# Seven products for every out block, first raw products in single banks, and a rewritten order of steps, in a fused attention and gated-unit kernel

## The chip, the cores and the metric

The kernel runs on one core of a Trainium2 chip. The metric is device time in microseconds (us) for one launch. Five engines work side by side, each on its own queue in strict program order: TensorE (PE, with weight loads listed as PEld), VectorE (DVE), ScalarE (ACT), GpSimd (POOL) and SyncE (SP, which here only issues transfers). They wait for one another by semaphores.

## What is computed

Eight batches, eight heads, 576 tokens, head size 64, all in fp32. First an attention without softmax, normalised per token and head; then a gated unit whose gate is a causal convolution over 5 tokens:

```
kv  = einsum('bhsd,bhse->bhde', k, v)
out = einsum('bhsd,bhde->bhse', q, kv)
x   = out / sqrt(mean(out*out, -1) + 1e-6) * g_norm     # heads side by side: (8, 576, 512)
gate = sigmoid(sum over taps k of conv_w[k] * x shifted by 4-k tokens)
result = (gate * (x @ w_val)) @ w_out                   # (8, 576, 512)
```

## The kernel before

**Tiling.** A batch `b` has five token chunks `c`: four of 128 tokens and one of 64. Channels are cut into four blocks `jt` of 128. Tokens lie strided, so that the convolution's shifts are shifts by 32 columns. The 64-token chunks of two batches share one out block; a pair of batches is numbered `i`, and its nine out blocks `c` 0 to 8.

**Steps.** Every piece of work is a small function, and a long list of step names, `PLAN`, calls them in an order written out in full (1151 steps). Engines follow that order strictly, so the list is the schedule. For one batch the steps are:

- `load_half`, `load_q`: k, v and q from memory (SP's queue). `turn_q` transposes q on VectorE (L458, L461); for batches 0 and 1 `turn_q_rows` does it on TensorE.
- `kv_product` (L438, TensorE) and `kv_copy` (ScalarE): k times v per head.
- `raw_product` (L493) or, from batch 2 on, `raw_pair` (L510): q times kv. A pair writes two chunks into a PSUM tile of two banks, `raws`. In batches 0 and 1 chunks 3 and 2 write one half each of the same tile.
- `square` (ScalarE), `sums` (L540, VectorE), `powers` (L546, GpSimd), `normalise` (ScalarE, 8 small activations; VectorE in batch 0).
- `turn_blocks` (L600, VectorE) and `move_blocks` (L608, four transfers from GpSimd's queue) bring x to channels by tokens, `xT`; `halo` copies the columns before it. Batches 0, 1 and the short chunks go by `turn_x` and `keep_x`.
- `gate_start` (L619, ScalarE), four `gate_tap` (L625, VectorE), `gate_end` (L632, ScalarE, sigmoid), `gated` (L650, VectorE: gate times value into `gv`).
- `val_product`, `keep_val` for batches 0 and 1; from batch 2 on the seven-product form: `x_sums` (L671, VectorE) forms sums of token halves, `val_fast` (L687) multiplies, `val_keep` copies or adds the results.
- `out_product` (L718, L725 for the shared short chunk) with `keep_out` (L733) for pairs `i` 0 and 1. For pairs 2 and 3 the seven-product form: `token_sums` (L758, VectorE), `fast_product` (L784, TensorE), `fast_keep` (L793 to L808: four copies on ScalarE and three adds on VectorE), with weight sums made once by `weight_sums`. Then `store`.

**The seven-product form.** Two out blocks of 128 tokens are one product of a 2 by 2 block matrix by a 2 by 2 block matrix. Instead of eight half-size products it makes seven, of sums and differences. A full block takes four products with 512 columns; a pair of blocks in the other form takes seven times two products with 256 columns. The number n of a `fast_product i p n` tells which of the seven, and p which pair of blocks.

**Buffers.** `gv` holds the gated values of three batches in turn. PSUM has eight banks: `raws` takes two, tag "tp" one and tag "mm" five, handed out by pools in the order of the calls; near the end `raws` is given back for two more. Work tiles (`gate` three, `ot` three, `x` two, `xs` four, `w64` three) come from pools too. The weights arrive in 64-bit form and are narrowed to fp32 by `narrow_weight` in eight small steps each, five on VectorE and three on ScalarE.

Of the kernel before, what the change touches and what calls it, by code (L numbers as in the profile page):

```python
# [15 lines left out]
P = 128  # L16
# [3 lines left out]
load_q_rows 0 1; stage_weight cw 0; load_q_rows 0 0; load_half v 0 0; load_half k 0 0; load_half v 0 1;  # L20
load_half k 0 1; warm_up; stage_weight wval 1; stage_weight wval 0; start_warm 36; turn_q_rows 0 0;
turn_q_rows 0 1; narrow_weight cw 0 0; turn_q_rows 0 2; narrow_weight cw 0 1; narrow_weight cw 0 2; sort_q 0 0;
turn_q_rows 0 3; sort_q 0 1; turn_q_rows 0 4; narrow_weight cw 0 3; kv_product 0 0; sort_q 0 2;
load_q_rows 1 0; narrow_weight cw 0 4; narrow_weight cw 0 5; load_half k 1 0; sort_q 0 3; narrow_weight cw 0 6;
load_half v 1 0; narrow_weight cw 0 7; sort_q 0 4; load_q_rows 1 1; load_half k 1 1; stage_weight wval 2;
keep_warm 2; kv_product 0 1; stage_weight wval 3; turn_cw; load_half v 1 1; kv_copy 0; keep_cw;
narrow_weight wval 1 0; raw_product 0 3; load_half v 2 0; raw_product 0 2; square 0 3; raw_product 0 4;
sums 0 3; stage_weight wout 0; square 0 2; raw_product 0 1; square 0 4; powers 0 3; sums 0 2;
narrow_weight wval 1 1; sums 0 4; raw_product 0 0; load_half v 2 1; square 0 1; narrow_weight wval 0 0;
narrow_weight wval 0 1; powers 0 2; square 0 0; normalise 0 3; sums 0 1; turn_x 0 3; sums 0 0; keep_x 0 3;  # L30
powers 0 4; normalise 0 2; narrow_weight wval 1 2; narrow_weight wval 1 3; turn_x 0 2; normalise 0 4;
turn_q_rows 1 0; roots 0; keep_x 0 2; narrow_weight wval 0 2; turn_x 0 4; sort_q 1 0; turn_q_rows 1 1;
keep_x 0 4; narrow_weight wval 0 3; normalise 0 1; turn_q_rows 1 2; halo 0; sort_q 1 1; normalise 0 0;
turn_x 0 1; narrow_weight wval 1 4; kv_product 1 0; narrow_weight wval 0 4; keep_x 0 1; sort_q 1 2;
narrow_weight wval 0 5; turn_x 0 0; narrow_weight wval 1 5; narrow_weight wval 0 6; turn_q_rows 1 3;
keep_x 0 0; narrow_weight wval 0 7; gate_start 0 0; turn_q_rows 1 4; narrow_weight wval 1 6; kv_product 1 1;
sort_q 1 3; load_q 2 0; narrow_weight wval 1 7; gate_start 0 1; narrow_weight wval 2 0; val_product 0 0 1;
gate_start 0 2; narrow_weight wval 3 0; sort_q 1 4; load_q 2 1; gate_tap 0 2 3; kv_copy 1; gate_tap 0 0 3;
narrow_weight wval 3 1; raw_product 1 3; narrow_weight wval 2 1; gate_tap 0 1 3; load_half k 2 0;
raw_product 1 2; keep_val 0 0 1; gate_tap 0 0 2; square 1 3; narrow_weight wval 3 2; val_product 0 1 1;  # L40
sums 1 3; square 1 2; gate_tap 0 1 2; powers 1 3; narrow_weight wval 2 2; load_half k 2 1; gate_tap 0 2 2;
narrow_weight wval 2 3; stage_weight wout 2; raw_product 1 1; sums 1 2; narrow_weight wval 3 3;
narrow_weight wval 2 4; raw_product 1 0; keep_val 0 1 1; powers 1 2; square 1 1; narrow_weight wval 2 5;
normalise 1 3; val_product 0 0 0; load_q 2 2; gate_tap 0 0 1; sums 1 1; turn_q 2 0; normalise 1 2; powers 1 1;
turn_x 1 3; narrow_weight wval 3 4; val_product 0 1 0; narrow_weight wval 2 6; keep_x 1 3; load_q 2 3;
narrow_weight wval 3 5; square 1 0; narrow_weight wval 2 7; normalise 1 1; turn_x 1 2; sums 1 0;
raw_product 1 4; gate_tap 0 2 1; stage_weight wout 1; powers 1 0; kv_product 2 0; narrow_weight wout 0 0;
square 1 4; sums 1 4; narrow_weight wout 0 1; narrow_weight wval 3 6; kv_product 2 1; keep_x 1 2; turn_q 2 1;
powers 1 4; normalise 1 0; gate_tap 0 2 0; turn_x 1 1; load_q 3 0; val_product 0 2 1; narrow_weight wval 3 7;
keep_x 1 1; gate_tap 0 1 1; keep_val 0 1 0; narrow_weight wout 0 2; gate_tap 0 1 0; keep_val 0 0 0; turn_x 1 0;  # L50
normalise 1 4; gate_tap 0 0 0; val_product 0 2 0; narrow_weight wout 2 0; narrow_weight wout 0 3; keep_x 1 0;
narrow_weight wout 0 4; kv_copy 2; val_product 0 3 1; turn_q 2 2; keep_val 0 2 1; keep_val 0 2 0; turn_q 2 3;
narrow_weight wout 2 1; load_q 3 1; gate_end 0 0; narrow_weight wout 0 5; turn_x 1 4; narrow_weight wout 0 6;
raw_pair 2 3; keep_val 0 3 1; keep_x 1 4; gated 0 0; narrow_weight wout 2 2; stage_weight wout 3; halo 1;
val_product 1 0 1; narrow_weight wout 0 7; load_q 3 2; square 2 3; square 2 2; sums 2 3;
narrow_weight wout 2 3; sums 2 2; powers 2 3; gate_end 0 1; val_product 1 0 0; narrow_weight wout 1 0;
gate_end 0 2; narrow_weight wout 2 4; gate_start 0 3; gated 0 1; keep_val 1 0 1; narrow_weight wout 2 5;
powers 2 2; load_half v 3 1; val_product 1 1 1; normalise 2 3; gate_tap 0 3 3; load_half k 3 0;
load_half v 3 0; turn_q 3 0; narrow_weight wout 2 6; val_product 0 3 0; normalise 2 2; gated 0 2;
narrow_weight wout 2 7; turn_blocks 2 3; narrow_weight wout 1 1; load_q 3 3; raw_pair 2 1; gate_tap 0 3 2;  # L60
narrow_weight wout 1 2; narrow_weight wout 3 0; raw_product 2 4; keep_val 1 0 0; turn_q 3 1; square 2 1;
val_product 1 1 0; load_half k 3 1; keep_val 0 3 0; sums 2 1; narrow_weight wout 3 1; gate_tap 0 3 1;
square 2 0; powers 2 1; square 2 4; sums 2 0; narrow_weight wout 3 2; val_product 1 2 1; gate_tap 0 3 0;
keep_val 1 1 1; narrow_weight wout 1 3; turn_blocks 2 2; powers 2 0; narrow_weight wout 3 3;
narrow_weight wout 1 4; val_product 1 2 0; normalise 2 1; turn_q 3 2; narrow_weight wout 3 4; load_q 4 1;
normalise 2 0; narrow_weight wout 3 5; val_product 1 3 1; narrow_weight wout 3 6; sums 2 4; load_q 4 0;
keep_val 1 1 0; narrow_weight wout 3 7; powers 2 4; gate_end 0 3; turn_blocks 2 1; kv_product 3 0;
gate_start 1 0; narrow_weight wout 1 5; keep_val 1 2 1; gated 0 3; normalise 2 4; val_product 1 3 0;
narrow_weight wout 1 6; gate_start 1 1; gate_tap 1 0 3; narrow_weight wout 1 7; turn_x 2 4; kv_product 3 1;
turn_blocks 2 0; keep_x 2 4; gate_start 1 2; gate_tap 1 0 2; move_blocks 2 3; keep_val 1 3 0; out_product 0 1;  # L70
turn_q 3 3; load_half k 4 1; kv_copy 3; load_half k 4 0; gate_tap 1 2 3; keep_val 1 3 1; keep_val 1 2 0;
gate_tap 1 1 3; gate_tap 1 0 1; gate_tap 1 1 2; raw_pair 3 3; gate_tap 1 0 0; gate_tap 1 1 1; out_product 0 0;
square 3 3; move_blocks 2 2; gate_tap 1 2 2; keep_out 0 1; gate_end 1 0; store 0 1; sums 3 3; square 3 2;
gate_tap 1 2 1; gated 1 0; powers 3 3; load_q 4 2; sums 3 2; out_product 0 3; keep_out 0 0; gate_tap 1 1 0;
gate_start 1 3; gate_tap 1 2 0; powers 3 2; gate_end 1 1; gate_tap 1 3 3; normalise 3 3; gate_tap 1 3 2;
move_blocks 2 1; store 0 0; out_product 0 2; gate_tap 1 3 1; gate_end 1 2; normalise 3 2; gated 1 1;
gate_tap 1 3 0; load_half v 4 0; halo 2; gated 1 2; gate_end 1 3; val_sums 0; raw_pair 3 1; keep_out 0 2;
gated 1 3; keep_out 0 3; turn_blocks 3 3; store 0 2; raw_product 3 4; square 3 1; val_sums 1; out_product 0 5;
square 3 0; move_blocks 2 0; turn_q 4 0; load_half v 4 1; sums 3 1; turn_blocks 3 2; val_sums 2; powers 3 1;
load_q 4 3; sums 3 0; out_product 0 7; turn_q 4 1; keep_out 0 5; square 3 4; powers 3 0; turn_q 4 2;  # L80
load_q 5 0; normalise 3 1; weight_sums 0; sums 3 4; val_sums 3; powers 3 4; normalise 3 0; out_product 0 4;
turn_blocks 3 1; x_sums 2 0; x_sums 2 1; gate_start 2 2; normalise 3 4; gate_tap 2 2 3; gate_start 2 0;
turn_blocks 3 0; kv_product 4 0; turn_q 4 3; gate_tap 2 2 2; kv_product 4 1; x_sums 2 3; turn_x 3 4;
x_sums 2 2; kv_copy 4; load_half k 5 1; val_fast 2 0 0; store 0 5; gate_tap 2 2 1; keep_x 3 4; raw_pair 4 3;
move_blocks 3 3; val_keep 2 0 0; val_fast 2 0 1; store 0 3; square 4 3; square 4 2; sums 4 3; val_fast 2 0 2;
gate_start 2 1; sums 4 2; powers 4 3; val_fast 2 0 3; load_half k 5 0; gate_tap 2 1 3; val_keep 2 0 2;
# [773 lines left out]
```

## Time and profile before

| | |
|---|---|
| time, median of 3 runs | 313.98 us (313.76 to 315.19) |
| span of the profiled execution | 313.7 us; the page lists no other time of it |
| granted TensorE clock | 1.000 |
| HBM read, written | 39.21 MB, 9.44 MB |
| `out_product` rows (L718) | 128 matmuls, 57.3 us busy; weight loads 190 ns |
| `gate_tap` rows (L625) | 128, 101.0 us busy, 810 ns each |
| `token_sums` rows (L758) | 16, 679 to 709 ns each |
| `fast_keep` adds (L793) | 24, about 420 ns each |

An fp32 product is listed as two matmuls, so 16 full out blocks of four products make the 128 rows. A row's mean is the length of one instruction; neighbours on an engine overlap a little, so the distance from one start to the next, in the timeline, is shorter than the mean, and an engine's busy time is less than the sum of its rows. The slices are fortieths of the span, 7.84 us each.

### The profile page before, as it was taken

What the parts mean: (1) busy time and instruction counts of PE and PEld (TensorE: products, weight loads), DVE (VectorE), ACT (ScalarE), POOL (GpSimd) and SP (SyncE); (2) the same over time, 40 slices, a digit from 0 to 9 for tenths busy, and PEclk for the clock granted to TensorE, in tenths of its full rate; (3) what the DMA queues carried; (4) which work ended last, traced back from release to release, by engine and by line L of the source; (5) the groups of instructions that cost most, each with busy time, mean ns of one, the idle gap of its engine ahead of it and who ended that gap; (6) DMA issues with size and microseconds to landing.
All of it is one profiled execution on the core that took longest, in us unless ns stands there. A gap on an engine that the chain in (4) does not pass through costs nothing.

```text
span 313.7 us, 8362 instructions
## 1 busy us (share of the span) xinstructions
PE 302.8 (97%) x3197; PEld 217.6 (69%) x3197; DVE 255.7 (82%) x462; ACT 191.1 (61%) x542; POOL 133.4 (43%) x175
## 2 busy tenths in 40 slices
PE   7978999999999999999999999999999999999993
PEld 7866878777645485757666776587668868888582
DVE  1149899999999969899999899899998999764412
ACT  1457899999485867747685858485773343352120
POOL 3033073435588456666684659265749000000000
PEclk9999999999999999999999999999999999999999
DMA  7999597599677769668966986422335213022322
GB/s 276 377 386 352 149 294 219 173 298 239 186 189 210 210 188 342 196 168 276 270 155 194 251 251 160 118 50 54 100 78 127 58 25 88 0 67 57 89 73 85
DMA packets 26696, 55.50 MB, mean 177 GB/s; under 512 B 6166, under 2 KB 8214, under 8 KB 26656
## 3 DMA queue, kind: packets, MB, share of 16 engines
q1 hardware_dynamic: 22608, 46.61, 49.8%
q0 software_dynamic: 3168, 6.32, 7.9%
q10 hardware_dynamic: 880, 2.03, 1.9%
q8 instruction: 25, 0.41, 0.5%
q14 instruction: 15, 0.12, 0.1%
HBM read 39.21 MB, written 9.44 MB: 155 GB/s over the span
## 4 chain that ended last, share of the span: by engine, by line
PE 85%; ACT 5%; DMA 4%; DVE 2%; SPq 1%; issue 1%; POOL 1%; ACTq 0%; DVEq 0%
PE out L718 18%; PE va L687 15%; PE a L784 8%; PE vc L687 8%; PE cb L784 6%; PE val L637 6%; PE raw L438 5%; PE out L725 5%; PE raw L510 4%; PE vb L687 4%; PE qTps L472 3%; PE raw L493 2%; DMA k<-in_k_dram 2%; DMA qs<-in_q_dram 2%; PE xTps L587 1%; ACT x L572 1%
## 5 line engine op out<-in xcount | busy, mean ns | idle before, releaser
L625 DVE SCALAR_TENSOR_TENSOR gate<-xT,cwT,gate 128x576 f32<-128x576 f32 x128 | 101.0, 810 | 2.1 <-ACT gate L619 1.6
L546 POOL TENSOR_TENSOR rt<-ss,mhalf 128x8 f32<-128x8 f32 (+1 forms) x38 | 65.4, 1728 | 80.7 <-DVE ss L540 77.1
L608 POOL DMA_DIRECT2D xT<-y x96 | 52.8, 556 | 17.4 <-DVE xs L671 6.0
L718 PE MATMUL out<-wout,gv 128*128 128x512 f32 x128 | 57.3, 595 | 0.0
L572 ACT ACTIVATE x<-raw,rt 128x64 f32<-128x64 f32 x252 | 55.3, 369 | 2.2 <-POOL rt L546 1.6
L718 PEld LDWEIGHTS out<-wout,gv 128*128 128x128 f32 x128 | 23.9, 190 | 26.0 <-issue 24.1
L637 PE MATMUL val<-xT,wval 128*128 128x288 f32 x128 | 32.9, 409 | 0.1
L540 DVE TENSOR_REDUCE ss<-sq 128x8 f32<-128x520 f32 (+1 forms) x38 | 23.3, 626 | 8.3 <-ACT sq L528 8.1
L528 ACT ACTIVATE sq<-raw 128x512 f32<-128x512 f32 (+1 forms) x40 | 21.6, 564 | 12.4 <-PE raw L510 8.8
L637 PEld LDWEIGHTS val<-xT,wval 128*128 128x128 f32 x128 | 23.6, 190 | 6.3 <-ACT xT L594 0.3
L619 ACT ACTIVATE gate<-xT,cwT 128x576 f32<-128x576 f32 x32 | 25.2, 796 | 4.0 <-DVE gv L650 3.9
L687 PE MATMUL va<-xs,vsum 128*128 128x288 f32 x96 | 27.2, 406 | 0.0
L650 DVE TENSOR_TENSOR gv<-gv,gate 128x576 f32<-128x576 f32 x32 | 24.2, 762 | 3.0 <-ACT gate L632 2.8
L632 ACT ACTIVATE gate<-gate 128x576 f32<-128x576 f32 x32 | 22.1, 702 | 5.5 <-DVE gate L625 5.4
L687 PEld LDWEIGHTS va<-xs,vsum 128*128 128x128 f32 x96 | 18.2, 190 | 4.7
L733 ACT COPY ot<-out 128x512 f32<-128x512 f32 x20 | 12.0, 603 | 14.0 <-PE out L725 6.0
L438 PEld LDWEIGHTS raw<-v,k 64*64 64x64 f32 x1008 | 15.5, 135 | 4.7 <-issue 3.8
L793 DVE TENSOR_TENSOR ot<-cb,ot 128x256 f32<-128x256 f32 x16 | 6.7, 420 | 14.7 <-ACT ot L797 7.0
L615 POOL COPY xT<-xT 128x124 f32<-128x124 f32 x32 | 13.4, 456 | 10.3 <-ACT xT L594 10.3
L708 ACT COPY gv<-va 128x288 f32<-128x288 f32 x12 | 4.8, 400 | 19.8 <-PE va L687 19.8
L438 PE MATMUL raw<-v,k 64*64 64x64 f32 x1008 | 16.8, 220 | 0.0
L600 DVE STREAM_TRANSPOSE y<-x 128x512 f32<-128x512 f32 x24 | 16.7, 698 | 0.0
(119 smaller groups left out, 516.7 us busy)
## 6 DMA issues: line engine op xcount, KB each, us to landing
qs<-in_q_dram SPq DMA_DIRECT2D x96, 140.0 KB, 4.3
out_dram<-ot SPq DMA_DIRECT2D x140, 64.0 KB, 2.3
k<-in_k_dram SPq DMA_DIRECT2D x14, 576.0 KB, 6.5
v<-in_v_dram SPq DMA_DIRECT2D x12, 576.0 KB, 6.3
xT<-y POOLq DMA_DIRECT2D x96, 64.0 KB, 3.4
y<-in_moe_w_val_dram SPq DMA_DIRECT2D x4, 512.0 KB, 12.0
w_wout<-in_moe_w_out_dram SPq DMA_DIRECT2D x4, 512.0 KB, 7.2
qs<-in_q_dram SPq DMA_DIRECT2D x3, 576.0 KB, 5.4
```

Of the source, the lines that this page charges most:

```text
L438: nc.tensor.matmul(raws[r * D:(r + 1) * D, s, i * D:(i + 1) * D], st["k", b, i][rows, r, cols], st["v", b, i][rows, r, cols], start=(j == ...
L540: nc.vector.reduce_sum(out=ss[:, 0:n], in_=st["sq", b, c][:, 0:n], axis=AX.X)
L546: nc.gpsimd.tensor_tensor(out=rt[:, 0:n], in0=st["ss", b, c][:, 0:n], in1=mhalf[:, 0:n], op=ALU.pow)
L572: nc.scalar.activation(out=x[:, to * D:(to + 1) * D], in_=one, func=AF.Copy, scale=st["rt", b, c][:, h:h + 1])
L608: nc.gpsimd.dma_start(out=xTs[b % 2][i * TB:(i + 1) * TB, :, first:first + P], in_=y[a * TB:(a + 1) * TB, i])
L619: nc.scalar.activation(out=gate[:], in_=xTs[b % 2][:, jt, HALO:SX], func=AF.Copy, scale=cwT[:, K - 1, jt:jt + 1])
L625: nc.vector.scalar_tensor_tensor(out=gate[:], in0=xTs[b % 2][:, jt, tap * TB:tap * TB + S], scalar=cwT[:, tap, jt:jt + 1], in1=gate[:], op ...
L637: nc.tensor.matmul(val[:], wval[:, kc, jt * P:(jt + 1) * P], xTs[b % 2][:, kc, HALO + n * SV:HALO + (n + 1) * SV], start=(kc == 0), stop=( ...
L650: nc.vector.tensor_tensor(out=both, in0=both, in1=st["gate", b, jt][:], op=ALU.mult)
L687: nc.tensor.matmul(st[bank, "val", b, mj][:], weights_[:, k], tokens()[:, k], start=(n in (0, 1, 3) and k == 0), stop=(k == NK // 2 - 1), ...
L718: nc.tensor.matmul(po[:], gv[:, jt, first:first + P], wout[:, jt, :], start=(jt == 0), stop=(jt == NK - 1),)
L784: nc.tensor.matmul(st[bank, i, p], tokens()[:, k], weights_[:, k], start=(n < 2 and k == 0), stop=(k == NK // 2 - 1), skip_group_check=True)
```

## The change

Pairs 0 and 1 get the seven-product form too, so 56 more `fast_product`, 16 more `token_sums` and 56 more `fast_keep` stand in the list, and 16 `out_product` with their `keep_out` are gone; the four shared short blocks stay as they were. Chunks 3 and 2 of batches 0 and 1 use a single bank each instead of halves of `raws`. The pools are replaced by fixed tiles, and the list says after an `@` which one a step's result takes. All steps are put in a new order (1247 steps); among them `weight_sums`, which now comes before the first out block, and `warm_up`, a sigmoid of one column, which stood near the head of the list and now stands in the middle. Functions for a further variant (`gate_side`, `gate_add`, seeded sums) are defined, but the list does not call them.

```diff
-load_q_rows 0 1; stage_weight cw 0; load_q_rows 0 0; load_half v 0 0; load_half k 0 0; load_half v 0 1;
-load_half k 0 1; warm_up; stage_weight wval 1; stage_weight wval 0; start_warm 36; turn_q_rows 0 0;
...
+stage_weight cw 0 @0; load_q_rows 0 1; load_q_rows 0 0; narrow_weight cw 0 0 @0; start_warm 36; turn_q_rows 0 2 @0;
+load_half k 0 0; load_half v 0 0; load_half v 0 1; narrow_weight cw 0 1; turn_q_rows 0 3 @1; narrow_weight cw 0 2;
...
+narrow_weight cw 0 7; sort_q 0 2; stage_weight wval 1; stage_weight wval 3; narrow_weight wval 1 0 @0; narrow_weight
+wval 1 5 @0; sort_q 0 1; load_q_rows 1 0; kv_copy 0; keep_warm 2; narrow_weight wval 1 1; narrow_weight wval 1 6;
+turn_cw @0; raw_product 0 4 @2; narrow_weight wval 3 5 @1; sort_q 0 0; narrow_weight wval 3 0 @1; raw_product 0 3
...
-square 3 0; move_blocks 2 0; turn_q 4 0; load_half v 4 1; sums 3 1; turn_blocks 3 2; val_sums 2; powers 3 1;
-load_q 4 3; sums 3 0; out_product 0 7; turn_q 4 1; keep_out 0 5; square 3 4; powers 3 0; turn_q 4 2;
...
+2; token_sums 0 0 0 @1; load_half k 3 1; load_half v 3 1; gate_start 1 1 @0; load_half v 3 0; normalise 2 0 @1;
+turn_blocks 2 1; keep_val 1 0 1; turn_blocks 2 0; powers 2 4 @0; gate_tap 1 1 3; keep_val 1 3 0; fast_product 0 0 0
...
-    BANKS = {"tp": 1, "mm": 5}
...
+    ROOMS = {"bank": 6, "gate": 3, "x": 2, "ot": 3, "wexp": 2, "w64": 3, "ss": 3, "rt": 3, "xs": 4, "sq": 2, "side": 0, "seed": 0}
+    PAIRED = range(2, 8)
+    SEED_VAL, PAIR_VAL = (), ()
+    SEED_OUT, PAIR_OUT = (), ()
...
+    def room(kind, *key):
+        if (kind, *key) not in st:
+            n = given.pop(0)
...
+            st[(kind, *key)] = rooms[kind][n]
+        return st[(kind, *key)]
...
     def raw_product(b, c):
         m = size(c)
-        if c in (3, 2):
-            raw = raws[:, 3 - c]
-        else:
-            raw = ps("tp" if b >= TURNED_X else "mm", [P, C], f"raw{b}_{c}")[:]
+        raw = room("bank", "raw", b, c)[:]
...
     def out_product(i, c):
-        po = ps("mm", [P, C], f"out{i}_{c}")
+        po = room("bank", "po", i, c)
...
+    def out_bank(bank, i, p):
...
+        both = room("bank", "out", "a" if bank == "a" else "cb", i, p)
+        return both[:, C // 2:] if bank == "b" else both[:, 0:C // 2]
```

## The prediction, made before the changed kernel ran

> **What bounds the kernel now.** I read the engines' totals and the forty slices first, then busy time in stretches of 10 us, the chain that ended last in order of time, and VectorE's timeline with its gaps. Totals, then slices:
>
> ```profile
> PE 302.8 (97%) x3197; PEld 217.6 (69%) x3197; DVE 255.7 (82%) x462; ACT 191.1 (61%) x542; POOL 133.4 (43%) x175
> ...
> PE   7978999999999999999999999999999999999993
> ...
> DVE  1149899999999969899999899899998999764412
> ```
>
> TensorE is busy 97% of the span, but VectorE's digits are 9 nearly as long; it is idle at both ends. The stretches, with PE, PEld, DVE, ACT and POOL in order:
>
> ```profile
> 60.00:70.00 10.00, 10.00 (x107) 7.70 (x107) 9.87 (x19) 9.95 (x30) 4.47 (x6) 1.00 0.99 295
> ...
> 110.00:120.00 10.00, 10.00 (x172) 7.53 (x165) 6.86 (x12) 6.46 (x20) 6.08 (x8) 1.00 0.78 235
> ...
> 280.00:290.00 10.00, 10.00 (x46) 8.36 (x44) 4.13 (x9) 3.80 (x10) 0.00 (x0) 1.00 0.20 51
> ```
>
> At 60 us three engines are full at once; at 110 only TensorE; after 280 VectorE is half empty. The chain of waits (start, us, what) prices one block both ways:
>
> ```profile
> 96.65 1.09 PE raw L510 x64
> 98.34 10.50 PE out L718 x24
> ...
> 243.11 0.86 PE a L784 x4
> 243.97 0.86 PE cb L784 x4
> ```
>
> Three full out blocks take 10.50 us with the change of shape in front of them, a single one 3.43 us in this view's steady rows; one of the seven products takes 0.863 us (243.97 less 243.11, and two in 1.73). VectorE's timeline gives its side (start, us, idle before it in brackets):
>
> ```profile
> 17.00 0.16 DVE L412 TENSOR_SCALAR gcol<-cwps 128x1 f32<-128x1 f32 x1 [5.10 <-PE cwps L408]
> ...
> 20.38 1.63 DVE L540 TENSOR_REDUCE ss<-sq 128x8 f32<-128x520 f32 x3 [2.42 <-ACT sq L528]
> ...
> 292.64 0.69 DVE L758 TENSOR_TENSOR sums<-sums,gv 128x512 f32<-128x512 f32 x1
> 293.25 0.68 DVE L758 TENSOR_TENSOR sums<-gv 128x512 f32<-128x512 f32 x1
> ```
>
> Adding all gaps of that timeline: VectorE has idled 20.3 us when the first `gated` ends at 59.3 us, 20.4 when `gated 1 3` ends at 97.36 us, 25.6 at `gated 3 3` (169.6 us) and 39.1 at the last one (288.7 us). So nothing is lost from 59 to 97 us: VectorE sets the pace there, and TensorE starts the blocks that need `gated 1 3` at 98.34 us, right behind it. From there TensorE runs without a gap to 309.05 us, and 4.65 us of last copy and store follow to 313.7. TensorE's rows from that block on sum to 207.3 us, against 210.7 on the clock: 1.6% goes to changes of shape. That factor is used below.
>
> The span is 313.7 us; no separate time of the profiled execution is listed, so 0.3 us, the distance to the median of 313.98, stands for what lies around it.
>
> **Part by part: TensorE.** Sixteen full blocks, eight pairs, become seven products each. Before, a pair is 2 x 3.43 = 6.87 us; after, 7 x 0.863 = 6.04. That removes 8 x 0.83 = 6.6 us. A product of 256 columns costs half of one of 512 (0.863 / 4 against 3.43 / 8), and its weight load, 190 ns, fits under a 216 ns pass.
>
> **VectorE.** Added are 16 `token_sums`. They start 0.61 us after one another where nothing waits (292.64 to 293.25), so 9.9 us. Added too are 24 adds of `fast_keep`, 420 ns long but 0.35 us apart: 8.4 us. `weight_sums` only moves. Total 18.3 us; busy goes from 255.7 to 274.
>
> **ScalarE.** Gone are 16 copies of 603 ns, added 32 of about 0.38: +2.5 us, and only after 75 us, where ScalarE is 50 to 80% busy. That hides it; uncovered it is 2.5 us. `warm_up`, which loaded the sigmoid's table at the start, now stands far down the list, and the built order has a second table load in front of the first `gate_end`. The load's row is 1.28 us and the next activation starts 10 ns after it (2.27 + 1.28, then 3.56), so I take 1.28 us; it falls near 50 us, where ScalarE is full, so up to 1.3 us of delay, zero if the order's slack there covers it. [...]
>
> **Rooms and first raw products.** The first two batches' chunks 3 and 2 leave the pair bank for single ones. The TensorE rows stay (0.49 us each), PSUM still has eight banks. Price: 0, down to -1.3 (the longest wait of PE for a bank or copy near 25 us) and up to +1.3 if a bank comes late instead. Stores of half-finished rows now wait on VectorE adds with q loads behind them on SP's queue. Loads land in 4.3 us and `turn_q` stands many steps later: 0, at worst one 4.3 us wait. GpSimd's steps are the same in number, moved among each other; it is busy 43% and waited 77 us for `ss`, which hides them, and uncovered one `powers` (1.87 us) would be late.
>
> **The start.** `kv_product 0 1` follows its sister directly (1.9 us of `keep_warm` now comes behind it), `raw_product 0 4` goes first, and five VectorE steps of weight narrowing (0.34 + 0.36 + 0.63 + 0.36 + 0.34 = 2.0 us) stand in front of the first `sums`, in the 5.10 us gap above. The weights land some 12 us after issue at 2.3 and 3 us, in time. With the 2.42 us gap mostly closed by the earlier small chunk (I take 1.9), 20.4 us of early idle become 16.5. Bounds: 20.4 (nothing gained) to 15.
>
> **The sum goes by VectorE, then TensorE.** In the new order, up to `gated 3 3` VectorE has: 64 taps x 0.738 = 47.2; eight weights narrowed x 2.565 = 20.5; 26 `sums` x 0.60 and 6 x 0.325 = 17.6; 20 `turn_q` x 0.75 = 15.0; 16 `gated` x 0.68 = 10.9; 16 `turn_blocks` x 0.627 = 10.0; 12 `x_sums` x 0.677 = 8.1; 13 `token_sums` = 8.0; 18 fast adds = 6.3; 14 value adds x 0.37 = 5.2; 8 weight or value sums x 0.60 = 4.8; first batch's normalising, roots and convolution weights 6.9. Together 160.5 us, by spacings where nothing waits. The same count for before gives 74.96 at `gated 1 3` where the clock less idle says 76.96; I add 2.5. Idle: 16.5, plus 2 for later waits (0 in the stretch where VectorE set the pace, 5.2 from 97 to 170 us where it did not). So `gated 3 3` ends at 160.5 + 2.5 + 18.5 = 181.5 us.
>
> `fast_product 1 3 0` needs it. From there TensorE has 70 products x 0.863 = 60.4, 46 `val_fast` x 0.97 = 44.6, three split blocks x 3.58 = 10.7 and 7.5 of raw, kv and turns: 123.2, x 1.016 = 125.2. End: 181.5 + 125.2 + 4.65 = 311.4 us. The same sum at the very last `gated`: 264.2 + 3.2 + 16.5 + 5 = 288.9, TensorE 17.4 x 1.016, and 4.65, gives 311.2. Both ends agree: VectorE is late for the whole middle, and TensorE's 6.6 us are mostly turned into waiting for it. With 0.3 around: **311.7, said as 311.8**.
>
> **Rivals.** (1) *TensorE stays the bound*, VectorE's early idle shrinking enough. For it: 58 us of VectorE idle, and 18.3 is less. Against it: most is at the ends, where nothing of the middle can go. Time: 313.98 - 6.6 = 307.4, less up to 3 of start: 304.4 to 307.4.
>
> (2) *Slower: VectorE's strict order waits as well.* An add or a `sums` stands in front of taps that could run, and waits for a product of a TensorE that itself waits for VectorE. The row is the 110 us stretch, 3.1 us lost in 10. Price: the 5.2 us lost from 97 to 170 instead of 2, and none of the start's 3.9: 311.7 + 3.2 + 3.9 = 318.8. It decides once idle before `gated 3 3` passes 22.5 us, which makes 315.7.
>
> (3) *The shorter products are not cheaper*: each change between products adds up to 0.2 us (1.06 against 0.86 behind 64-row groups). 33 of 56 new products so placed eat the 6.6 us: 313 to 315.5. Against it: neighbours of other kinds in the chain show 0.86 throughout.
>
> **How the numbers follow.** A measurement here tells about 0.5% from no change: 1.57 us, so faster is below 312.4, slower above 315.55. Forecast 0.5 (own range 309.2 to 314.7, by idle of 16 to 21.5): 0.3 faster, 0.17 same, 0.03 slower. Rival 1: 0.2, faster. Rival 2: 0.25, of which 0.03 same. Rival 3: 0.05, same. Faster 0.5, same 0.25, slower 0.25. The range 306 to 318.5 leaves out the best of rival 1 and the worst of rival 2.
>
> **What would show it.** Right: VectorE busy near 274, its slices 9 almost to the last `gated`, which ends near 289; its idle before `gated 3 3` 16 to 21; TensorE busy near 296 with gaps between 100 and 290 us whose releasers are VectorE lines (`gated`, `token_sums`, `x_sums`); two table loads. Wrong: TensorE without a gap from 60 us on (rival 1), VectorE idle spread through the middle behind PE or ACT rows (rival 2), products above 0.9 us (rival 3).

## The result: slower, and the profile after

| | before | after |
|---|---|---|
| time, median | 313.98 us | 326.22 us (322.43 to 333.87, 5 runs) |
| ratio to before | | 1.034 [1.028, 1.040] |
| profiled execution: time, span, clock | span 313.7, clock 1.000 | 322.43, 320.5, 0.989 |
| TensorE busy, idle before its last row | 302.8, 6.2 us | 298.5, 17.0 us |

The forecast of 311.8 us was wrong, and the time lies outside its range (306 to 318.5). Ratios leave out executions more than 1.5% above the fastest of their kernel, medians are over all, and three experiments (VectorE's load with two buffers, later first readers, half of the transfers from ScalarE) have a profile of such an execution, so that its waits are read below and its total time is not. The four other runs of after have clocks of 0.964 to 0.978. Totals and slices of after:

```profile
span 320.5 us, 8626 instructions
...
PE 298.5 (93%) x3293; PEld 238.0 (74%) x3293; DVE 271.4 (85%) x502; ACT 194.0 (61%) x559; POOL 140.3 (44%) x175
...
PE   7999989999879999699799994999899999999993
...
DVE  1289999999969999799989896499899999999621
...
PEclk9999999999999999999999998799999999999999
```

TensorE has less to do, as the sum had it, but its row of nines has holes, the deepest a 4 in the slice from 192 to 200 us, and there and in the next slice the granted clock falls to 8 and 7. Before, it ran from 60 to 160 us without a pause; after, it is busy 91.9 us of these 100. Its timeline (start, us, rows, idle before in brackets) gives the three largest waits:

```profile
90.23 2.18 PE L708 MATMUL bank<-xT,wval 128*128 128x288 f32 x8 [3.11 <-DMA xT<-y]
...
131.42 3.15 PE L708 MATMUL bank<-xT,wval 128*128 128x288 f32 x12 [3.12 <-ACT x L585]
...
199.02 6.03 PE L708 MATMUL bank<-xT,wval 128*128 128x288 f32 x12 [4.07 <-DMA xT<-y]
```

All three stand in front of the first `val_fast` of a batch (2, 3 and 5): the first reader of `xT`, which `move_blocks` fills. The releaser named at 131 us is not one that this `val_fast` waits for: its bank had been emptied by 127.99 us. The last of batch 3's transfers landed at 131.12 us, 0.30 us before the product, and VectorE's `x_sums`, the other first reader, began at 131.39. In front of the other two waits the last landings are at 89.93 and 198.72 us, again 0.30 us before. Twelve such matmuls take 3.15 us behind the second wait and 6.03 behind the third: half speed. The chain that ended last shows what runs in front of the third wait (start, us, what):

```profile
179.18 0.43 DVE ot L809
179.60 0.33 issue
179.94 0.60 POOL xT L621
...
180.54 2.73 POOL xT L621 x6
...
184.35 3.71 POOL rt L560 x2
188.07 0.56 POOL xT L621
...
188.63 3.24 POOL xT L621 x6
191.87 6.85 DMA xT<-y
198.72 0.30 issue
199.02 6.04 PE bank L708 x12
```

Read it from below. TensorE waits for transfers; they took 6.85 us to land in the chain; sixteen issues on GpSimd, 0.55 us each, had two `powers` (3.71 us) between them; and the first issue began 0.7 us after VectorE had passed the last tap of batch 3 (178.45 to 179.26 us), whose buffer batch 5 overwrites. (The chain names the row behind that tap.) From the first issue to the first product that is 19.1 us.

**Where the time went.** The spans differ by 6.8 us: TensorE's busy time fell by 4.3 and its idle time rose by 10.8 (together 6.5; the end is 0.3 longer). In a run at clock 0.999 (below) it is busy 295.7, so the removed work is 7.1 us, and 2.8 us of it came back as slower rows. Span times (1 - clock) is 3.5 us in the profiled run, and 7.1 to 12.0 in the others: by this sum the clock accounts for nearly all of the 3.8 us by which the median is longer than the profiled run. The other runs have no profile that would show their waits.

### The profile page after: what moved, and what is told of

It is laid out like the page before. It is cut to its first block, busy times and chain, and to the rows that moved or that the text cites. A ratio compares the mean times of both kernels' runs of the same rounds, so it can differ in the third digit from the quotient of the medians.

```text
span 320.5 us, 8626 instructions
## 1 busy us (share of the span) xinstructions
PE 298.5 (93%) x3293; PEld 238.0 (74%) x3293; DVE 271.4 (85%) x502; ACT 194.0 (61%) x559; POOL 140.3 (44%) x175
## 4 chain that ended last, share of the span: by engine, by line
PE 43%; DVE 21%; ACT 10%; DMA 9%; POOL 7%; issue 7%; SPq 1%; DVEq 0%; ACTq 0%; POOLq 0%
PE bank L796 20%; PE bank L708 11%; DVE gate L637 5%; ACT x L585 4%; POOL rt L560 4%; DMA qs<-in_q_dram 3%; PE end L708 3%; POOL xT L621 2%; DVE gv L669 2%; PE raw L462 2%; DMA v<-in_v_dram 2%; DMA xT<-y 2%; DVE ss L554 2%; PE bank L491 2%; DMA out_dram<-ot 2%
## 5 line engine op out<-in xcount | busy, mean ns | idle before, releaser
L796 PE MATMUL bank<-wsum,w 128*128 128x256 f32 x192 | 48.2, 384 | 2.5 <-ACT ot L812 2.5
L796 PEld LDWEIGHTS bank<-wsum,w 128*128 128x128 f32 x192 | 35.8, 190 | 11.1 <-ACT ot L812 3.4
L708 PE MATMUL bank<-xT,wval 128*128 128x288 f32 x84 | 26.3, 452 | 10.3 <-DMA xT<-y 7.2
L708 PE MATMUL bank<-xs,vsum 128*128 128x288 f32 x128 | 35.2, 407 | 0.0
L657 PE MATMUL bank<-xT,wval 128*128 128x288 f32 x128 | 33.3, 411 | 1.5 <-ACT gv L665 1.4
L809 DVE TENSOR_TENSOR ot<-bank,ot 128x256 f32<-128x256 f32 x48 | 19.6, 414 | 16.5 <-PE bank L796 7.4
L796 PE MATMUL bank<-wout,gv 128*128 128x256 f32 x128 | 32.2, 380 | 0.0
L657 PEld LDWEIGHTS bank<-xT,wval 128*128 128x128 f32 x128 | 23.6, 190 | 7.9 <-ACT gv L665 1.7
L708 PEld LDWEIGHTS bank<-xT,wval 128*128 128x128 f32 x84 | 17.2, 211 | 15.8 <-issue 7.9
L708 PEld LDWEIGHTS bank<-xs,vsum 128*128 128x128 f32 x128 | 24.2, 190 | 5.8
L796 PEld LDWEIGHTS bank<-wout,gv 128*128 128x128 f32 x128 | 24.4, 191 | 4.2 <-DVE y L613 0.2
L542 ACT ACTIVATE sq<-raw 128x512 f32<-128x512 f32 x24 | 14.5, 623 | 7.9 <-PE raw L525 7.8
```

Source lines behind the costliest of these rows:

```text
L657: nc.tensor.matmul(val, wval[:, kc, jt * P:(jt + 1) * P], xTs[b % 2][:, kc, HALO + n * SV:HALO + (n + 1) * SV], start=(kc == 0), stop=(kc ...
L708: nc.tensor.matmul(val_bank(bank, b, mj), weights_[:, k], tokens()[:, k], start=(n in (0, 1, 3) and k == 0 and not seeded), stop=(k == NK ...
L796: nc.tensor.matmul(out_bank(bank, i, p), tokens()[:, k], weights_[:, k], start=(n < 2 and k == 0), stop=(k == NK // 2 - 1), skip_group_che ...
```

## The experiments

Theory A: the new list starts the moves so late before their first readers that transfers which were hidden are not hidden any more. Theory B, the prediction's: VectorE's 18.3 us more set the pace. Theory C: granted clock lost behind the waits adds to either. The kernel before was timed again beside the experiments (medians 314.61 to 314.97 us), and each ratio is to those times.

### A third buffer for xT

```diff
-    xTs = [const.tile([P, NK, SX], FP32, name=f"xT{i}") for i in range(2)]
+    xTs = [const.tile([P, NK, SX], FP32, name=f"xT{i}") for i in range(3)]
+    rooms["wexp"] = rooms["xs"][2:4]     # makes the space
...
-xTs[b % 2]
+xTs[b % 3]
```

> The changed kernel with three xT buffers in place of two (two small tiles share others' room for it). Theory 1a (the moves of batch 5 stand behind the last tap of batch 3, which still reads the buffer): the 4.1 us wait near 199 us goes with the 3 us of low clock behind it, span 313 to 317 us; the waits near 90 and 131 us stay, since there the moves wait for turn_blocks. Theory 1b (the moves wait for the GpSimd queue or the transfers, not for the buffer): nothing changes, span 320 to 325 us.

Measured: 316.27 us median of 10, ratio to before 0.999 [0.995, 1.003]; the profiled run 312.82, span 311.0, clock 0.999. Its totals:

```profile
PE 295.7 (95%) x3293; PEld 235.4 (76%) x3293; DVE 271.0 (87%) x506; ACT 193.8 (62%) x559; POOL 139.7 (45%) x175
...
PEclk9999999999999999999999999999999999999999
```

```profile
170.29 4.41 POOL L622 DMA_DIRECT2D xT<-y  x8 [1.30 <-PE raw L463]
...
193.14 3.07 PE L709 MATMUL bank<-xT,wval 128*128 128x288 f32 x12
```

The moves of batch 5 start at 170.3 instead of 179.9 us, and the wait near 199 us is gone. TensorE's idle time is 10.4 us. Of the two waits that were expected to stay, the one at batch 2 did (2.57 us); at batch 3 there is none in this execution, where the last transfer landed 17.5 us after the first issue instead of 19.2. A buffer, without any other step moved, gives back nearly all of the loss.

### VectorE's load, with three buffers and with two

```diff
     def token_sums(i, h, n):
...
+        if i < 2:
+            return
...
+        total = lambda s: chunk(s // 2, EVEN) if i < 2 else lambda: out_sums(i, h, s)[:, :, m, :]
...
+        add = lambda out, one, two: None if i < 2 else nc.vector.tensor_tensor(out=out, in0=one, in1=two, op=ALU.add)
```

The `token_sums` and adds of pairs 0 and 1 are left out, and their products read plain tokens in place of the sums.

> The changed kernel with the third xT buffer, and of the new work for pairs 0 and 1 VectorE's part left out: 16 token_sums and 24 adds, 18.3 us of VectorE by the prediction's count (the products take plain tokens in place of the sums). If VectorE's load sets the end directly, as the prediction has it, TensorE becomes the bound: 304 to 308 us. If with a third buffer TensorE runs at its own pace but for the waits for the second table load and for batch 2's transfers, the time stays within 2 us of the run with the third buffer alone: 309 to 314, with VectorE's busy time near 253 and its idle time grown by as much.

> The changed kernel with its two xT buffers, and VectorE's part of the new work for pairs 0 and 1 left out (16 token_sums, 24 adds, 18.3 us; the products take plain tokens in place of the sums). If VectorE's load is what lets the last taps free the xT buffer late, the moves of batches 3 and 5 start several us earlier, TensorE's waits of 3.1 and 4.1 near 131 us and 199 us shrink to under 1.5 each, and the time is 314 to 319 us. If the order of the list holds the buffer whatever VectorE's load is (each step waits for the one written before it), the waits stay within 1 us of what they were: 322 to 327.

Measured, three buffers: 315.41 us, ratio 1.000 [0.997, 1.003], where 304 to 308 was B's number. VectorE is busy 255.3, and its last `gated` stands where it stood. The two timelines, third buffer alone and then with VectorE's new work left out:

```profile
287.07 1.63 DVE L670 TENSOR_TENSOR gv<-gv,gate 128x576 f32<-128x576 f32 x2 [0.39 <-ACT gate L653]
```

```profile
287.36 1.63 DVE L670 TENSOR_TENSOR gv<-gv,gate 128x576 f32<-128x576 f32 x2 [0.39 <-ACT gate L653]
```

Sixteen us of work gone, and the last `gated` 0.3 us later: VectorE's idle time up to it grew from 23.3 to 39.1 us. It was following, not leading. With two buffers: 324.34 us median of 4, ratio 1.021 [1.014, 1.028] against 1.034 [1.028, 1.040] for after, and the waits at batches 2 and 5 are still there (3.94 and 4.71 us); the one at batch 3 is not.

```profile
206.85 3.35 PE L708 MATMUL bank<-xT,wval 128*128 128x288 f32 x7 [4.71 <-DMA xT<-y]
```

By the middles of the ratios VectorE's load is worth some 4 us there, by their intervals anything from nothing to 8; these runs do not settle it closer. The moves of batch 5 start 16.5 us before TensorE comes to their reader, where in after they start 15.0 us before: 1.5 us gained, not the several that were expected, so VectorE's load is at most a small part of what makes them late. B, by which the time had to follow VectorE's load, falls.

### GpSimd's order

```diff
-move_blocks 3 2; move_blocks 3 3; powers 4 2; powers 4 3; powers 4 4; move_blocks 3 0; move_blocks 3 1
+move_blocks 3 2; move_blocks 3 3; move_blocks 3 0; move_blocks 3 1; powers 4 2; powers 4 3; powers 4 4
```

(GpSimd's steps alone; the same for batch 5 and the `powers` of batch 6.)

> The changed kernel with two xT buffers as it is; only GpSimd's order differs: the last two move_blocks of batch 3 and of batch 5 stand directly behind the first two, ahead of the `powers` that stood between them. If the queue on GpSimd is a large part of the transfers' lateness, TensorE's waits near 131 us and 199 us (3.1 and 4.1) shrink to under 1.5 each, and the clock holds there: 317 to 321 us. If only the late release of the buffer by VectorE's last taps counts, the waits stay as they are: 324 to 327. A rival on the other side: the `powers`, now 4.4 us later, hold back the norms of batches 4 and 6, and TensorE waits for their raw banks instead: 325 to 330.

Measured: 327.17 us, ratio 1.038 [1.035, 1.040]. GpSimd's, ScalarE's and TensorE's timelines:

```profile
122.03 4.33 POOL L621 DMA_DIRECT2D xT<-y  x8 [2.70 <-DMA xT<-y]
126.38 4.45 POOL L560 TENSOR_TENSOR rt<-ss,mhalf 128x8 f32<-128x8 f32 x3
```

```profile
129.69 1.74 ACT L585 ACTIVATE x<-raw,rt 128x64 f32<-128x64 f32 x8 [4.21 <-POOL rt L560]
```

```profile
131.75 2.07 PE L796 MATMUL bank<-wsum,w 128*128 128x256 f32 x4 [5.08 <-ACT ot L812]
```

The rival that had been written for the other side came true. The first readers of batches 3 and 5 no longer wait, their last transfers having landed 7.8 and 4.9 us before them; batch 2's, whose moves were left as they were, waits 3.02 us. But the second eight issues now wait for transfers, `powers` begins at 126.4 instead of 116.4 us, ScalarE waits 4.21 us for it with copies queued behind, and TensorE waits 5.08 us for those. Before batch 5's readers the same happens at a `raw_pair`, which waits 5.20 us. Both kinds of GpSimd step are on the path here; the two orders tried only choose which wait it is.

### Later first readers

```diff
-val_fast 5 0 3; val_fast 5 1 0; x_sums 5 1; val_fast 5 0 0; fast_product 1 3 3; ... fast_product 1 3 4; ... fast_product 1 3 5
+fast_product 1 3 3; ... fast_product 1 3 4; ... fast_product 1 3 5; val_fast 5 0 3; val_fast 5 1 0; x_sums 5 1; val_fast 5 0 0
```

(Here for batch 5; the same for 2 and 3.)

> The changed kernel with two xT buffers, its GpSimd order and its VectorE load; only the first readers of the moved x stand later in the list: for batches 2, 3 and 5 the first three val_fast, with the x_sums and copies that belong to them, go behind two to four TensorE steps that were to follow anyway (3.7, 2.6 and 2.6 us of work). By the cover theory that is cover added for nothing: the waits of 3.1, 3.1 and 4.1 us near 90, 131 and 199 us shrink to 0.5, 0.5 and 1.5 or less, the clock holds, and the time is 311 to 317 us. If the waits come from elsewhere (landing slowed by other transfers, or VectorE), they move along with the readers and the time stays at 322 to 327. Rival on the way: val_keep and x_sums, later by as much, make TensorE wait at the following val_fast, and half is given back: 317 to 321.

Measured: 321.81 us median of 4, ratio 1.019 [1.014, 1.025]. TensorE's timeline:

```profile
91.30 1.16 PE L525 MATMUL raw<-kvbd,qT 64*64 64x64 f32 x64 [1.86 <-ACT x L585]
...
133.49 2.91 PE L708 MATMUL bank<-xT,wval 128*128 128x288 f32 x11 [0.65 <-issue]
...
202.65 4.84 PE L708 MATMUL bank<-xT,wval 128*128 128x288 f32 x12 [2.30 <-DMA xT<-y]
```

In front of the first readers 3.11, 3.12 and 4.07 us of waiting became 0, 0.65 and 2.30: TensorE work put in front of a reader takes the place of its wait. (The twelve matmuls behind the last still run slowly, 4.84 us.) But a `raw_pair`, now ahead of the readers, waits 1.86 us itself, and another new wait of 2.60 us stands in front of 160.7: half is given back, as the rival of this run had it.

### A shorter chain: half of the transfers from ScalarE's queue

```diff
+            queue = nc.scalar if (b, a) in ((2, 3), (2, 1), (3, 0), (3, 1), (5, 1), (5, 0)) else nc.gpsimd
-            nc.gpsimd.dma_start(
+            queue.dma_start(
```

> The changed kernel with two xT buffers and its order; of the moves of batches 2, 3 and 5 the later two of each batch (eight transfers) are issued from ScalarE's queue instead of GpSimd's. By the cover theory TensorE has 12.6 (batch 2), 17.0 (3) and 16.0 us (5) of listed work between the step that lets the moves start and the first product that reads them, against 17 to 20 us of issuing, `powers` between, and landing. Eight issues less in the row, 4.4 us, should close the waits near 90, 131 and 199 us to under 1 us each, and GpSimd's next `powers` come 4.4 us earlier: 312 to 317 us. If landing, not issuing, is the long part, the waits shrink by less than 1 us each: 322 to 327. A rival: the issues hold ScalarE (eight times up to 0.55 us) and TensorE waits for its copies instead: 318 to 323.

> Third xT buffer, warm_up at the head, no idle products, and the later two moves of batches 2 and 3 issued from ScalarE's queue. If the cover theory holds, the 2.7 us and 4.0 us waits that the third buffer leaves in some runs near 89 and 131 us are gone, the clock stays at 0.995 or more, and without the idle products' 2.6 us of work each run is 309 to 311.5, below the version with them. If ScalarE's issues cost what they save: 312 to 315.

Measured: two buffers 321.32 us median of 4, ratio 1.013 [1.010, 1.016]: better than after. Of TensorE's waits, batch 3's reader has none left (its neighbours wait 1.36 and 1.19), batch 5's has 0.86; batch 2's grew to 5.34. ScalarE's timeline shows why:

```profile
83.24 1.11 ACT L542 ACTIVATE sq<-raw 128x512 f32<-128x512 f32 x2
84.09 4.11 ACTq L622 DMA_DIRECT2D xT<-y  x4
```

At batch 2 ScalarE came to its last four issues 84.1 us into the run, when GpSimd alone would have been through (83.8 us in after), and these four took 4.11 us, 1.03 each, against 0.55 on GpSimd; over all 24 that ScalarE made, the row of an issue is 0.61 us in the median. With the third buffer, `warm_up` at the head and the halves of batches 2 and 3 on ScalarE: 318.44 us, 1.014 [1.011, 1.016], and 5.61 us of waiting at batch 2. So issuing from ScalarE helped at batches 3 and 5 (0 and 0.86 us of waiting left) and hurt at batch 2 (5.34 instead of 3.11), where ScalarE came to it late.

### The clock

```diff
+fill 4 3; val_fast 2 1 0 @4 ... +fill 2 3; val_fast 3 1 0 @2 ... +fill 0 3; val_fast 5 0 3 @0
+    def fill(bank, n):
+        for _ in range(n): nc.tensor.matmul(rooms["bank"][bank][:], ident[:], wout[:, 0, :], start=True, stop=True)
```

> The changed kernel with three idle products (2.6 us, results overwritten) in front of the first val_fast of batches 2, 3 and 5, so that TensorE is not idle while x arrives. Theory 3 (part of the loss is the granted clock, which falls after a long wait): clock 1.000 in every run, span near 317 us and within 1 us from run to run. Rival (the clock does not matter, or falls for another reason): span 320 to 325 us and a clock below 0.99 as before.

Measured: 321.44 us, ratio 1.020 [1.014, 1.027], clock 0.995 to 1.000 in every run, spans 317.6 to 321.3. The time from the work in front of a wait to the first reader is left about as it was, and products whose results are overwritten still took 4.8 us off the median. C holds, as far as the clock goes. The expected agreement within 1 us was missed: two runs at clock 1.000 have spans of 318.1 and 321.3 us, so part of the spread between runs is not clock. And in front of batch 5 the idle products did not keep the clock up in the profiled run: twelve matmuls took 4.83 us there (last section).

### The table load, and full blocks in the new order

```diff
-load_half ... warm_up (in the middle of the list)
+warm_up (first in the list)
```

> The changed kernel with warm_up at the head of the list, so that the second table load (1.28 us at 43 us on a full ScalarE) goes. If it stands on the path: the 1.4 us wait of TensorE near 45 us goes and the time falls by 1.3 to 2.7 us. If ScalarE makes it up later: no change.

Measured: 323.68 us, 1.025 [1.017, 1.033]. The wait of 1.42 us near 45 us is gone, those at 90 and 200 us are not (3.01, 4.78). The medians differ by 2.5 us, as expected for a load on the path, but the intervals of the two ratios overlap, and the two profiled spans, at clocks of 0.988 and 0.989, differ by 0.7 us: whether the rest is absorbed further on stays open.

```diff
-fast_product i p 0..6, fast_keep i p 0..6, token_sums i h 0..3   (i = 0, 1)
+out_product i c, keep_out i c                                     (i = 0, 1)
```

> The new order and rooms with pairs 0 and 1 as full blocks again: 18.3 us of VectorE work out, 6.6 us of TensorE work back in. Theory 1 (VectorE is late, whoever then waits for it): the TensorE waits in front of the first val_fast of batches 2, 3 and 5 (3.1, 3.1 and 4.1 us) go, the granted clock is 1.000, and the time is 311 to 316 us. Theory 2 (the new order itself is bad): the waits stay and the time is 322 us or more.

Measured: 336.98 us, 1.072 [1.066, 1.077]. The waits in front of the first readers are nearly gone (0.47 us at batch 2, none at 3 and 5), which Theory 1 expected, but the time is over 20 us above its range; the 322 or more of Theory 2 was to come with those waits. Two lines of the waits of this kernel, both on other engines than TensorE:

```profile
ACT sq L525 <- PE raw L508: 29.3, 9, 11.1
...
DVE ss L537 <- ACT sq L525: 24.7, 9, 9.1
```

ScalarE waits 29 us in all for raw products and VectorE 25 us for ScalarE behind them. A reading that fits, and that no run shows, is that blocks of 3.4 us in places made for products of 0.86 us hold up the raw products. An order written for one form does not fit the other, so this is no clean undo and decides nothing about VectorE.

### Towards a better version

Each has the third buffer and `warm_up` at the head, unless said otherwise.

| kernel | time | ratio to before |
|---|---|---|
| moves of 3 and 5 ahead of `powers`, batch 2's chunk 3 moved last | 316.04 | 1.003 [1.001, 1.006] |
| later readers for 2 and 3 | 315.94 | 1.004 [1.001, 1.007] |
| nothing more | 313.69 | 0.995 [0.991, 0.998] |
| idle products before batches 2 and 3, `warm_up` left where it was | 314.16 | 0.999 [0.995, 1.002] |
| idle products before batches 2 and 3 | 312.98 | 0.994 [0.992, 0.997] |

> Third xT buffer, warm_up at the head, the moves of batches 3 and 5 ahead of the `powers`, and batch 2's move of chunk 3 (which its first products do not read) last of its four. If what is left after the third buffer is 1.4 us behind the table load, 2.6 us behind batch 2's transfers and some clock lost by them, the span is 306 to 309 and the time 308 to 311, under the kernel before. If the gains are given back further on, as with warm_up alone, it stays at 312 to 316.

> Third xT buffer, warm_up at the head and the later first readers for batches 2 and 3, no idle products. By the cover theory the waits of 2.7 and 4.0 us that the third buffer with warm_up alone had in its profile are gone without the 2.6 us of idle products: 309 to 311.5, clock 0.995 or more, the fastest so far. If the delay is given back behind it: 312 to 314.

> Third xT buffer and warm_up at the head, without the idle products. If the idle products make the gain of the run with all three (312.98), this one has clocks of 0.98 to 0.995 in part of its runs and 314 to 317 us. If the table load at the head makes it, it comes to 311.5 to 313.5 as well.

> Third xT buffer and the idle products in front of the first val_fast of batches 2 and 3, with warm_up left where the changed kernel has it. If the idle products make the gain, the clock is 0.995 or more in all runs and the time 312 to 315, the 1.4 us wait behind the table load remaining. If both are needed, 315 to 318.

> Third xT buffer, warm_up at the head, and three idle products of 0.86 us in front of the first val_fast of batches 2 and 3, to keep TensorE's clock up where it waits. If the spread of the third buffer's runs (clock 0.977 to 1.000) comes from TensorE's waits before these products, all runs stay at a clock of 0.995 or more and within 1% of each other: 311 to 314. If the clock drops for another reason, the spread stays, 312 to 322.

The last one is ahead of both kernels, by 0.6% of the one before: seven of its eight executions took 311.60 to 314.18 us, one 1609.54. Its interval overlaps that of "nothing more", so what the idle products add is not settled. Its totals and clock:

```profile
PE 298.7 (96%) x3305; PEld 235.7 (76%) x3305; DVE 270.9 (87%) x506; ACT 192.4 (62%) x558; POOL 139.0 (45%) x175
...
PEclk9999999999999999999999999999999999999998
```

TensorE's idle time is 6.6 us, near the 6.2 of before; of its busy time some 5 us are the six idle products (three took 2.74 us in the run with two buffers; the 2.6 us of the expectations is one group). Without them, a run can be as fast (311.04) or lose clock again: the profiled run has a wait of 4.01 us at batch 3, and twelve matmuls of 4.83 us behind it. Reordering GpSimd, or the readers, on top of the third buffer misses its range (308 to 311, 309 to 311.5) in both cases: the first again waits for `powers` (4.35 us at 126 us), the second gives the delay back at the `raw_pair` (2.07 us).

## Why the prediction was wrong

**The step that failed** is the sentence on GpSimd: steps "the same in number, moved among each other", on an engine that "waited 77 us for `ss`, which hides them". So the term was 0, at worst one `powers` of 1.87 us; it measured 10.3 us of TensorE waits (3.11, 3.12, 4.07), and clock behind them. The waiting of an idle engine was taken for cover of its transfers. What covers a transfer is the work that its reader's engine has between the release and the read, and that could have been counted from the two lists, with TensorE's durations (0.863 us a fast product, 0.97 a `val_fast`, 3.43 a full block, and so on), before any run. How slowly the transfers would land could not. From the last step that holds the moves back (the batch's last `turn_blocks`, or the last tap on the buffer they overwrite) to the first `val_fast`, TensorE has by the list:

| batch | 2 | 3 | 4 | 5 | 6 | 7 |
|---|---|---|---|---|---|---|
| before, us | 29.4 | 32.1 | 29.3 | 34.3 | 33.6 | 27.4 |
| after, us | 12.6 | 17.0 | 17.1 | 16.0 | 18.1 | 18.5 |
| first issue to last landing, after | 14.9 | 19.2 | 12.7 | 18.8 | 15.2 | 10.9 |
| more than the cover | 2.3 | 2.2 | | 2.8 | | |
| TensorE's wait | 3.11 | 3.12 | 0 | 4.07 | 0 | 0 |

The new list halves the cover, and the three batches whose transfers take longer than it are the three that wait. With 0.7 us from the step that holds the moves back to the first issue, and 0.3 from the last landing to the first product, as in all three, the sums are 3.3, 3.2 and 3.8 us, within 0.3 of the waits.

Landing has its share. From the last issue to the last landing it took 6.7, 6.1 and 6.9 us in these three batches, and 2.0 to 2.7 in the other three; before, 2.0 to 3.8 in all six. With the landing of before, an estimate by the same sum is 0 to 0.5 us of wait: the halved cover left nothing to spare, and slower landing used it up. No run moved the loads and stores that ran beside these transfers, so what made them land later stays open.

The cover also says what the third buffer can do: for batch 5 the last tap no longer counts and the cover becomes 22.8 us, against 19.8 from first issue to last landing; for batches 2 and 3 `turn_blocks` holds the moves and nothing changes (12.6, 17.0). That fits the wait that went (199 us), the one that stayed (2.57 us at 89.9), and the one that comes and goes between runs (131 us).

**The pace.** "VectorE is late for the whole middle, and TensorE's 6.6 us are mostly turned into waiting for it" fell with the two light runs. The sum took VectorE's idle time as given and added work to it. In the run with a third buffer, and no wait for the moves of batch 5, the span of 311.0 is the predicted end of 311.4, and the last `gated` ends at 288.7 where 288.9 was said. That is coincidence: the same `gated` ends at 289.0 with 16 us less VectorE work. In after itself it ends at 298.2.

**The terms.** TensorE's -6.6 measured -7.1. VectorE's +18.3 measured +15.7 (271.4 less 255.7; 16 times 0.61 is 9.8, not 9.9, which matters little). ScalarE's +2.5 measured +2.9. VectorE's idle time at the start, put at 16.5 us, was some 14; its later waits up to `gated 3 3`, put at 2, were some 9. The table load takes 1.28 us in after (from 43.27 us) and the next activation starts 0.02 us behind it, at 44.57, so the length that was taken from the row was right; but the load was on the path, with 1.42 us of TensorE waiting. The 0.3 us around the span was too little: in after's profiled run 322.43 less 320.5 is 1.9, and the other runs show 1.8 to 1.9.

**The rivals.** Rival 2 had the right sign, and its own condition was just met (VectorE idle some 23 us before `gated 3 3`, over 22.5), but its mechanism, VectorE waiting behind TensorE, is not what the runs show, and its 318.8 had no clock in it. Rival 1, TensorE as the bound, describes the runs with a third buffer, where VectorE's load did not matter; but no run reached its 304.4 to 307.4. The fastest single one took 311.04. An estimate of the least is some 307 us: TensorE's 295.5 us of work (the least in any of the profiles), some 5 of its waits at the start, the 4.65 of the end and 1.8 around the span.

**The clock** was in no term. In after, waits of 3.11 and 3.12 us left the next products at full speed. Behind the wait of 4.07 us the twelve products lost 6.03 less 3.15, 2.9 us: the trace has the clock at half from 198.02 to 204.85 us, of which TensorE idled the first 1.0. Shorter waits cost clock in other runs (last section).

## What to carry to other kernels

When a list is reordered, count for every transfer the work of the reader's engine between the step that frees its buffer and its first read, before and after, and set it against issuing plus landing; idle time of the issuing engine says nothing about that. An engine that is busy nearly all the time may still only be following, as VectorE here: with 15.7 us less work its last `gated` ended 0.3 us later, and its idle time grew by 15.8. A TensorE wait can cost twice, once as the wait and once as clock: waits of 2.30, 2.59, 3.02 and 4.07 us did here, and 2.57, 3.11 and 3.12 did not. A few idle products in front of such reads may be worth more than they cost: with two buffers they took 4.8 us off the median.

## What the runs showed of the hardware that was not expected

TensorE's clock can read half behind a wait. In after it read 0.50 from 198.02 to 204.85 us, behind the wait at batch 5, and 1.00 in and behind the waits at batches 2 and 3 (stretch, its length, TensorE busy, clock, DMA share, GB/s):

```profile
87.12:90.23 3.11, 0.00 (x1) 1.00 0.84 217
90.23:92.20 1.97, 1.97 (x8) 1.00 0.08 25
128.30:131.42 3.12, 0.00 (x0) 1.00 1.02 303
131.42:134.57 3.15, 3.15 (x13) 1.00 0.91 299
194.95:198.02 3.07, 0.00 (x0) 1.00 0.96 236
198.02:204.85 6.83, 5.83 (x12) 0.50 0.04 12
204.85:208.00 3.15, 3.15 (x16) 1.00 0.00 0
```

The rows grew with it: 12 matmuls in 6.03 us instead of 3.15. In the run with GpSimd's order changed, 64 small ones (`raw_pair`) took 1.99 instead of 1.16 behind a wait of 5.20. The length of the wait alone does not decide. In that run eight matmuls took 4.18 us behind 3.02 us of waiting at batch 2, where in after they took 2.18 behind 3.11. In the run with idle products and two buffers, 2.59 us of listed waiting, right behind six idle matmuls, were followed by twelve products of 4.83 us in all, and the 2.30 us in the run with later readers by 4.84; with the third buffer 2.57 us cost nothing, the clock of that run being 0.999. The run with idle products:

```profile
195.42 2.74 PE L459 MATMUL bank<-wout,ident 128*128 128x512 f32 x6
200.75 4.83 PE L714 MATMUL bank<-xT,wval 128*128 128x288 f32 x12 [2.59 <-DMA xT<-y]
```

What else decides is not shown. Nor is it shown that one wait is free in one execution of a kernel and dear in the next, which would fit the spread between its runs: each kernel has one trace.

Transfers of 64 KB from GpSimd's queue, 3.2 us from issue to landing in the median, took 6.7, 6.1 and 6.9 us at the end of the three late chains, where loads and stores ran beside them (DMA share 0.84, 1.02 and 0.96 in the stretches above): that is a third of the chain or more. That those slow them is a guess that no run tests; in the run with GpSimd's order changed, the last of batches 3 and 5 still took 5.7 and 7.0 us.
